# Dividing attention's product with v by the softmax sums, spread over rows by TensorE, in the first five visits

## The chip, the cores and the metric

The kernel runs on one core of a Trainium2 chip. Five engines work side by side, each through its own queue in order: TensorE (PE) multiplies matrices into PSUM, VectorE (DVE), ScalarE (ACT) and GpSimd (POOL) work elementwise (POOL does not read PSUM in this kernel), and SyncE (SP) issues DMA transfers. The metric is the device time of one execution in microseconds; lower is better.

## What is computed

Attention in which a query sees only those keys whose hash (the signs of six random projections) falls into the same bucket, then a two-layer network with squared relu on the joined heads.

```python
q_bits = (np.einsum('bhsd,dk->bhsk', q, proj) > 0).astype(np.int64)
k_bits = (np.einsum('bhsd,dk->bhsk', k, proj) > 0).astype(np.int64)
mask = q_bucket[:, :, :, None] == k_bucket[:, :, None, :]
scores = np.where(mask, scale * np.matmul(q, k.transpose(0, 1, 3, 2)), -1e9)
attn = np.exp(scores - np.max(scores, axis=-1, keepdims=True))
attn = attn / (np.sum(attn, axis=-1, keepdims=True) + 1e-09)
x = np.matmul(attn, v)            # 4 batches, 8 heads, 768 rows, 64 wide
h = np.maximum(x_rows @ w_in, 0)  # x_rows is 3072 x 512, w_in 512 x 2048
out = h * h @ w_out               # w_out 2048 x 512
```

## The kernel before

**Visits and units.** A visit is one batch, one pair of heads and one third (256) of the query rows; there are 48 (line 1039). A visit has four units, one for each head and 128 rows (`unit`, line 877): scores S into PSUM (tiles `pS`, `side`), their maximum on DVE (`line`), the exponential on ScalarE with its row sums (`e`, `sm`), and the sums' reciprocal `rv` (one operation on POOL or DVE, then one on DVE). `prep` (line 782) makes the masked operands A, L, Q, M of a pair of heads from the loaded k and q: a hash on PE (`pd` or `side` with `pj`), its signs `bits` on ScalarE, and rows of mask through PE (`side` or `pc`) that DVE and ScalarE copy to the lower halves of A, L, Q, M.

**Two ways from e to the product with v.** In a plain visit (line 907; `PLAIN_AV`, the first four) e is divided in place by POOL (`move(e, e, rv, ...)`, with `DIVIDE = ("pool",)`), PE transposes it in float32 in two halves (`pT`, against the unit matrix `unit_f`), ScalarE or DVE copies each half to `aT`, and `av` (line 925) multiplies with the float32 V, 12 matmuls with the two heads beside each other. In the other visits e is divided into two float16 parts (`hl`, one on ScalarE and one on DVE, lines 917 and 918), a DMA transpose on SP's queue brings them to `aT`, and `av` takes 36 float16 matmuls with the split `VV`. The product is copied out of the bank `pA` as two float16 parts `xx`.

**The network.** When all four pairs of heads of a third are done, `moe` (line 981) multiplies `xx` with `win` (into `pm`), squares on ScalarE and DVE (`g`), and multiplies with `wo` (into `po`). The weights arrive while the first visits run: `fetch` (line 665) loads a 512-wide block, copies its upper 16 bits (`move(first..., (dve, pool))`, line 671, room<-room in the profile) and joins the lower bits on DVE; `split` (line 692) squares it for a scale (`sq`) and writes two float16 parts into `win` or `wo`.

**What sets the order.** All operations are recorded (`Program.add`) and ordered when the kernel is built. An operation may have several ways, one for each engine that can do it. `forward` takes at each step the operation of the lowest priority number that can start and picks the engine that ends it first by planned costs; the priorities come from a first schedule (`rounds`) and are then changed at random, once for each number in the table `PATH` (`shake`). `SOON` scales the planned duration of transfers until `SOON_TO`. Thus the same operations come out in another order, and partly on other engines, wherever an operation or a number changes. All operations are issued from one helper, line 565 (558 for groups of matmuls, 563 for chains), which is why the profile shows that line for nearly all.

**The tiles of the first units.** `unit_f` is loaded on SP's queue (line 647), and `ident`, a cast of it on DVE (line 649), is needed for the scale of V (`dg`). `idle` are matmuls without use that fill PE's waits at the beginning.

Of the kernel before, what the change touches and what calls it, by code (L numbers as in the profile page):

```python
# [12 lines left out]
F16 = mybir.dt.float16  # L13
BF16 = mybir.dt.bfloat16
# [10 lines left out]
P = 128  # L25
# [24 lines left out]

ROUNDS, BEHIND = 24, 40000
PATH = (
# [13 lines left out]
)  # L66
LOADS = 0

# [3 lines left out]

PLAIN, PLAIN_TO, ALTERNATE, DOUBLE = 4, 12, 16, 34

PLAIN_AV, DIVIDE = (0, 1, 2, 3), ("pool",)

AV_RUN = 18

# [15 lines left out]

SWITCH, ENTRY = 95, 105
TRANSPOSES, HBM, SMALL = 165, 265, 300
SOON, SOON_TO = 0.7, 22000


class Buffer:  # L100
# [477 lines left out]
def lsh_attention_moe(ctx: ExitStack, tc, kq, v, proj2, w_in, w_out, consts, out):  # L578
# [64 lines left out]
    for n in range(4):  # L643
        move(sgn[32 * n : 32 * n + 32, n * P : (n + 1) * P], both_f[0:32, 4:], 1.0, (dve, pool) if n else (dve,))
    pr.rank = 0.0
    unit_f = sb([P, P], F32, "unit_f")
    sp.dma_start(unit_f, consts[:, 4 + 2 * P :])
    ident = sb([P, P], BF16, "ident")
# [16 lines left out]
    def fetch(src):  # L665

        raw = place(turn[0] % 2 * 4096, 4096, U32).rearrange("p (n t) -> p n t", t=2)
        send(raw.rearrange("p n t -> p (n t)").bitcast(U16)[:, 0:2047], src.bitcast(U16)[:, 1:2048])
        first = tops[turn[0] % len(tops)]
        turn[0] += 1  # L670
        move(first[:, :, 1], raw.rearrange("p n t -> p (n t)").bitcast(BF16).rearrange("p (n t) -> p n t", t=4)[:, :, 2], 1.0, (dve, pool))
        f = place(12288 + turned[0] % ((ROOM - 12288) // 2048) * 2048, 2048, F32)
        turned[0] += 1
        dve.scalar_tensor_tensor(f.bitcast(U32), raw[:, :, 0], 13, first.rearrange("p n t -> p (n t)").bitcast(U32), ALU.logical_shift_right, ALU.bitwise_or)
        return f
# [198 lines left out]
        return VV  # L874


    def unit(st, part, i, aT, plain):
        c0 = part * PT + i * P
        u = pr.rank
        if u >= DOUBLE and u % 2:  # L880
            pS = side
        else:
            pS = ps([P, 2, 512], F32, "pS", tag="po" if u % 2 and u < ALTERNATE else "pS")
        pr.marks[u] = len(pr.ops)
        pr.rank = u - 1000
        for s, (a, bb) in enumerate(st):
            for j in range(2):
                pe.matmul(pS[:, j, 0:HS], a[:, c0 : c0 + P], bb[:, j * HS : (j + 1) * HS], start=s == 0, stop=s == len(st) - 1)
        sS = pS[:, 0:2, 0:HS]
        line = lines[int(u) % 2]  # L890
        nmx = line[:, 1:2]
        todo = [("tensor_reduce", (nmx, sS, AX.XY, ALU.max), {"negate": True})]
        to = {"bias": nmx}
        if len(st) > 1:
            pair = sb([P, 2], F32, "pair", 2)
            todo += [("scalar_tensor_tensor", (pair, nmx.broadcast_to([P, 2]), MASK * MASK / 2, line, ALU.is_lt, ALU.mult), {})]
            to = {"scale": pair[:, 0:1], "bias": pair[:, 1:2]}
        pr.add((dve, "chain", todo, {}))
        e = sb([P, S], F32, "e", BUFS["e"])
        sm = sb([P, 1], F32, "sm", 2)  # L900
        act.activation(e.rearrange("p (j s) -> p j s", j=2), sS, AF.Exp, accum_out=sm, **to)
        pr.rank = u
        rv = sb([P, 1], F32, "rv", 3)
        pr.add(*[(q, "tensor_scalar", (rv, sm, 1e-9, 1.0 if plain else 1.0 / ASC, ALU.add, ALU.mult), {}) for q in (dve, pool)])
        dve.reciprocal(rv, rv)
        if plain:
            move(e, e, rv, tuple(getattr(pr, k) for k in DIVIDE))
            for g in range(2):
                pT = ps([P, 512], F32, "pT", tag=("pm", "pA")[g])[:, 0:HS]
                pr.busy_from = min(pr.busy_from, len(pr.ops))  # L910
                for c in range(3):
                    kc = 3 * g + c
                    pe.matmul(pT[:, c * P : (c + 1) * P], e[:, kc * P : (kc + 1) * P], unit_f, start=True, stop=True, is_transpose=True)
                move(aT[:, 3 * g : 3 * g + 3, i * P : (i + 1) * P], pT.rearrange("p (c s) -> p c s", c=3), 1.0, (act, dve))
            return
        hl = sb([P, 2, S], F16, "hl", BUFS["hl"])
        move(hl[:, 0], e, rv)
        left(hl[:, 1], e, rv, hl[:, 0])
        sp.dma_start_transpose(aT[:, :, i * P : (i + 1) * P], hl.rearrange("p t s -> p (t s)"))
# [2 lines left out]

    xxs = {}

    def av(b, hp, part, VV, aTs):
        pA = ps([P, 512], F32, "pA")[:, 0:PT]
        plain = VV.dtype == F32
        todo = [(kc, t * D, kc + l * KC) for t, l in (((0, 0),) if plain else ((0, 0), (1, 0), (0, 1))) for kc in range(KC)]
        scale = vscales[b][0] if plain else 1.0 / ASC
        run = []  # L930
        for n, (kc, d0, c) in enumerate(todo):
            run += [((pA[m], VV[:, h, kc, d0 : d0 + D], aTs[h][:, c]), {"start": n == 0, "stop": n == len(todo) - 1}) for h, m in enumerate((T, U))]
            if (n + 1) % (AV_RUN if not plain else 6) == 0:
                pr.add((pe, "matmuls", run, {}))
                run = []
        xx = xxs[b, part, hp] = sb([P, 2, PT], F16, "xx")
        move(xx[:, 0], pA, scale)
        left(xx[:, 1], pA, scale, xx[:, 0])

# [113 lines left out]
    done, u, stages = {}, 0, 0  # L1053
    for n, (b, hp, part) in enumerate(visits):
        sts, aTs, plain = kept[b, hp], [], n in PLAIN_AV
        for h, st in enumerate(sts):
            aT = sb([P, KC, PT], F32, "aT") if plain else sb([P, 2 * KC, PT], F16, "aT")
            aTs.append(aT)
            for i in range(RT):
                pr.rank = now[0] = u  # L1060
                unit(st, part, i, aT, plain)
                u += 1
        if n + 1 < len(visits):
            ready(*visits[n + 1][:2], u + PREP, n + 1 < PLAIN_TO and visits[n + 1][1] < PLAIN)
        if (b, hp, plain) not in kept_v or not alive([kept_v[b, hp, plain]]):
            pr.rank = u - 2 * RT + PREP
            kept_v[b, hp, plain] = values(b, hp, plain)
        pr.rank = u - 0.5
        av(b, hp, part, kept_v[b, hp, plain], aTs)
        if n in early:  # L1070
            do, j, pr.rank = early[n]
            do(j)
        done[b, part] = done.get((b, part), 0) + 1
        if done[b, part] == H // 2:
            moe(stages, b, part)
            stages += 1
# [35 lines left out]
```

## Time and profile before

| | us |
|---|---|
| median of 3 runs (lowest, highest) | 869.69 (867.09, 871.51) |
| the profiled execution | 867.13 |
| its span, first to last instruction | 865.1 |
| PE, DVE, ACT, POOL busy | 832.1, 661.7, 666.0, 111.5 |

The span is what the trace covers; the execution's own time is 2.0 us longer. Rows of the profile read: line, engine, operation, written tile <- read tiles, shapes, count, then busy time, the mean ns of one, and the engine's idle time just before them with what ended it. A table of windows gives each engine's busy time in a stretch of the span, the granted clock of TensorE (PEclk, 1.00 is full) and the DMA engines' share. In the chain of waits each piece is a start, a length and what ran.

### The profile page before, as it was taken

Reading aid. Unit: us, or ns where it says so; the run is one execution under the profiler, and the core shown is the slowest. Engines: PE = TensorE matmul, PEld = TensorE weight load, DVE = VectorE, ACT = ScalarE, POOL = GpSimd, SP = SyncE. Lnnn points to the kernel's source line nnn. Section 1 sums busy time; section 2 is a strip of 40 time slices with the busy share of each in tenths; the row PEclk is TensorE's granted clock in tenths of the full one; section 3 lists DMA queues with packets and bytes.
Section 4 is the critical chain, followed back from the end, with each engine's and each line's share of the span. In section 5 each row is a group of like instructions: output and inputs, shape, how many; then the busy total and the mean of one; then the engine's idle time right before and its main releaser. Section 6 shows DMA issues by size and latency. Waiting matters only on the chain.

```text
span 865.1 us, 16996 instructions
## 1 busy us (share of the span) xinstructions
PE 832.1 (96%) x6340; PEld 543.8 (63%) x6343; DVE 661.7 (76%) x1448; ACT 666.0 (77%) x1153; POOL 111.5 (13%) x175
## 2 busy tenths in 40 slices
PE   6999978998999999999999999999999999999997
PEld 4555555665566667667666667676666666766664
DVE  4889988999696999877796888885887988871111
ACT  3897867699796888877886898977887888883332
POOL 0554464310010100000000001000100000000000
PEclk8999999999999999999999999999999999999999
DMA  8426979865788898787575978797665798771000
GB/s 298 128 82 185 195 197 226 188 117 108 177 168 189 159 166 163 143 156 169 134 156 153 165 155 146 151 159 164 135 111 157 145 150 150 135 147 38 1 25 25
DMA packets 301634, 125.77 MB, mean 145 GB/s; under 512 B 279792, under 2 KB 287728, under 8 KB 301552
## 3 DMA queue, kind: packets, MB, share of 16 engines
q1 hardware_dynamic: 301264, 124.61, 68.6%
q8 instruction: 50, 0.82, 0.4%
q14 instruction: 32, 0.26, 0.1%
q10 hardware_dynamic: 288, 0.08, 0.0%
HBM read 37.36 MB, written 6.29 MB: 50 GB/s over the span
## 4 chain that ended last, share of the span: by engine, by line
PE 73%; DVE 11%; ACT 8%; issue 3%; DMA 3%; POOL 1%; SPq 0%; ACTq 0%; DVEq 0%; POOLq 0%
PE pm L565 24%; PE po L565 24%; PE pA L558 9%; PE pS L565 8%; PE side L565 6%; DVE line L563 3%; ACT e L565 3%; DVE hl L565 2%; ACT g L565 1%; ACT hl L565 1%; PE pd L558 1%; DMA unit_f<-consts 1%; DMA V<-vp 1%; DVE room L565 1%; PE pc L565 1%
## 5 line engine op out<-in xcount | busy, mean ns | idle before, releaser
L565 PE MATMUL pm<-xx,win 128*128 128x256 f16 x2304 | 308.3, 273 | 3.0 <-DVE g L565 1.2
L565 PE MATMUL po<-wo,g 128*128 128x512 f16 x1152 | 298.7, 379 | 4.7 <-ACT acc L565 3.2
L565 PEld LDWEIGHTS <-win 128*128 128x128 f16 x2304 | 223.0, 98 | 84.0 <-issue 18.0
L565 DVE SCALAR_TENSOR_TENSOR hl<-e,rv,hl 128x768 f16<-128x768 f32 x176 | 179.5, 1025 | 15.8 <-ACT hl L565 14.8
L565 PEld LDWEIGHTS <-g 128*128 128x128 f16 x1152 | 111.4, 98 | 107.6 <-issue 11.2
L565 ACT ACTIVATE hl<-e,rv 128x768 f16<-128x768 f32 x168 | 155.2, 928 | 8.3 <-DVE rv L565 3.8
L563 DVE TENSOR_REDUCE line<-pS 128x1 f32<-128x768 f32 x113 | 107.8, 954 | 21.0 <-PE pS L565 18.9
L565 ACT ACTIVATE g<-g 128x512 f32<-128x512 f32 (+1 forms) x184 | 114.7, 625 | 10.3 <-PE po L565 7.7
L565 POOL TENSOR_SCALAR rv<-sm 128x1 f32<-128x1 f32 x98 | 37.9, 387 | 590.5 <-ACT e L565 558.3
L565 DVE SCALAR_TENSOR_TENSOR g<-g,g 128x512 f16<-128x512 f32 x84 | 57.7, 686 | 69.1 <-ACT g L565 69.0
L565 ACT ACTIVATE g<-pm 128x512 f32<-128x512 f32 x93 | 55.0, 591 | 68.6 <-PE pm L565 68.5
L558 PE MATMUL pA<-aT,VV 128*64 128x256 f16 x1584 | 94.9, 274 | 0.0
L558 PEld LDWEIGHTS <-VV 128*64 128x64 f16 x1584 | 83.1, 110 | 12.9 <-issue 12.5
L565 ACT ACTIVATE e<-pS,pair 128x768 f32<-128x768 f32 x72 | 71.0, 986 | 24.0 <-DVE pair L563 13.8
L565 ACT ACTIVATE e<-side,pair 128x768 f32<-128x768 f32 x72 | 71.0, 986 | 12.6 <-DVE pair L563 7.3
L563 DVE TENSOR_REDUCE line<-side 128x1 f32<-128x768 f32 x79 | 75.2, 951 | 5.0 <-PE side L565 4.0
L565 ACT ACTIVATE e<-pS,line 128x768 f32<-128x768 f32 x41 | 36.9, 899 | 8.3 <-DVE line L563 6.8
L565 PEld LDWEIGHTS <-room 128*128 128x128 f16 x288 | 27.8, 98 | 18.3 <-issue 1.3
L565 PE MATMUL pS<-A,L 128*128 128x384 f32 x84 | 34.9, 529 | 4.6 <-DVE L L565 2.4
L565 PE MATMUL pS<-room 128*128 128x384 f16 x144 | 36.0, 326 | 0.0
L565 PE MATMUL side<-room 128*128 128x384 f16 x144 | 34.6, 326 | 0.0
L565 PE MATMUL pS<-Q,M 128*128 128x384 f32 x80 | 31.3, 503 | 2.5 <-ACT e L565 2.3
(164 smaller groups left out, 905.6 us busy)
## 6 DMA issues: line engine op xcount, KB each, us to landing
R<-kq SPq DMA_DIRECT2D x24, 384.0 KB, 4.1
room<-w_in SPq DMA_DIRECT2D x16, 511.8 KB, 3.9
room<-w_out SPq DMA_DIRECT2D x16, 511.8 KB, 3.7
V<-vp SPq DMA_DIRECT2D x16, 384.0 KB, 4.1
out<-acc SPq DMA_DIRECT2D x24, 256.0 KB, 2.8
room<-room SPq DMA_DIRECT2D x60, 96.0 KB, 2.9
aT<-hl SPq DMA_TRANSPOSE x176, 3.9
Q<-kq SPq DMA_DIRECT2D x6, 384.0 KB, 4.1
```

Source lines behind the costliest of these rows:

```text
L558: ins = q.engine.matmul(*map(real, args), **kw).ins
L563: issue(q, getattr(q.engine, name)(*map(real, args), **{k: real(x) for k, x in kw.items()}).ins)
L565: ins = getattr(q.engine, o.name)(*map(real, o.args), **{k: real(x) for k, x in o.kw.items()}).ins
```

## The change

In the first five visits (the fifth is new: `PLAIN_AV` gets a 4) e goes undivided through the float32 transposes and the product with V. For each unit a diagonal matrix with rv on it is made from `unit_f` (`DIVIDE` is now ScalarE; the four diagonals of a visit lie in one `hl` buffer). In `av`, four float32 matmuls of ones (128 x 64) with the diagonals put each row's reciprocal sum into all 64 partitions of the output, in the free half of the bank `pA`; a copy scales them by V's scale, and DVE multiplies the product with them before it is split into `xx`. The upper-bits copy of a weight block may now also go to ScalarE; second halves of transposes keep `pA`, and from unit 16 on first halves use it too. `SOON` no longer shortens early transfers, and `PATH` is another, longer table (2,564 numbers for 234).

```diff
 PATH = (
-    400004, 400029, 400036, 400042, 400059, 400060, 400072, 400092, 400101, 400104, 400119, 400137, 400139, 400148, 400157, 400162, 400198, 400206,
...
+    1200002, 1200003, 1200004, 1200005, 1200006, 1200007, 1200008, 1200014, 1200015, 1200017, 1200018, 1200019, 1200020, 1200024, 1200029, 1200031,
...
-PLAIN_AV, DIVIDE = (0, 1, 2, 3), ("pool",)
+PLAIN_AV, DIVIDE = (0, 1, 2, 3, 4), ("act",)
...
-SOON, SOON_TO = 0.7, 22000
+SOON, SOON_TO = 1.0, 0
...
+    ones_f = sb([P, D], F32, "ones_f")
+    pool.memset(ones_f, 1.0)
...
-        move(first[:, :, 1], raw.rearrange("p n t -> p (n t)").bitcast(BF16).rearrange("p (n t) -> p n t", t=4)[:, :, 2], 1.0, (dve, pool))
+        move(first[:, :, 1], raw.rearrange("p n t -> p (n t)").bitcast(BF16).rearrange("p (n t) -> p n t", t=4)[:, :, 2], 1.0, (dve, pool, act))
...
-    def unit(st, part, i, aT, plain):
+    def unit(st, part, i, aT, plain, dg=None):
...
-            move(e, e, rv, tuple(getattr(pr, k) for k in DIVIDE))
+            move(dg, unit_f, rv, tuple(getattr(pr, k) for k in DIVIDE))
             for g in range(2):
-                pT = ps([P, 512], F32, "pT", tag=("pm", "pA")[g])[:, 0:HS]
+                pT = ps([P, 512], F32, "pT", tag="pm" if g == 0 and u < 16 else "pA")[:, 0:HS]
...
-    def av(b, hp, part, VV, aTs):
-        pA = ps([P, 512], F32, "pA")[:, 0:PT]
+    def av(b, hp, part, VV, aTs, dgs=None):
+        bank = ps([P, 512], F32, "pA")
+        pA = bank[:, 0:PT]
...
+        if plain:
+            pR, t, rvs = bank[:, PT:], dgs[:, 0:PT], dgs[:, 2 * RT * P :]
+            matmuls(*[(pR[m, i * P : (i + 1) * P], ones_f, dgs[:, (h * RT + i) * P : (h * RT + i + 1) * P]) for i in range(RT) for h, m in enumerate((T, U))])
+            move(rvs, pR, scale, (act, dve))
...
         xx = xxs[b, part, hp] = sb([P, 2, PT], F16, "xx")
+        if plain:
+            dve.tensor_tensor(t, pA, rvs, ALU.mult)
+            move(xx[:, 0], t)
+            left(xx[:, 1], t, 1.0, xx[:, 0])
+            return
         move(xx[:, 0], pA, scale)
         left(xx[:, 1], pA, scale, xx[:, 0])
...
+        dgs = sb([P, 2, S], F16, "hl", BUFS["hl"]).rearrange("p t s -> p (t s)").bitcast(F32) if plain else None
```

Three places show what the order becomes. First, SP's queue at the start of the program, where the loads are issued (A and Q are k and q of a head, V two heads of v, room<-w_in a block of weights). Before:

```order
L565 DMA Q<-kq 128x768
L565 DMA A<-kq 128x768 x2
L565 DMA Q<-kq 128x768
L565 DMA V<-vp 128x768
L565 DMA room<-w_in 128x2047
L565 DMA V<-vp 128x768
L565 DMA room<-w_in 128x2047
L565 DMA V<-vp 128x768 x2
L565 DMA Q<-kq 128x768
L565 DMA A<-kq 128x768
L565 DMA unit_f<-consts 128x128
```

And of the change:

```order
L713 DMA A<-kq 128x768
L713 DMA Q<-kq 128x768 x2
L713 DMA A<-kq 128x768
L713 DMA room<-w_in 128x2047
L713 DMA unit_f<-consts 128x128
L713 DMA room<-w_in 128x2047
L713 DMA V<-vp 128x768 x4
L713 DMA Q<-kq 128x768
```

The load of unit_f stood thirteenth and stands sixth now, ahead of all four loads of v.

Second, DVE's queue in the first two visits' preparation, up to the first maximum (L, M, A, Q<-side are the mask rows, room<-room the join of a weight's bits, line_78 and line_63 the maximum of the first unit). Before:

```order
L565 TENSOR_SCALAR L<-A 64x768
L565 TENSOR_SCALAR M<-Q 64x768
L565 TENSOR_SCALAR A<-side 64x384 x2
L565 TENSOR_SCALAR L<-side 64x384
L565 TENSOR_SCALAR room<-room 128x512
L565 CAST ident<-unit_f 128x128
L565 SCALAR_TENSOR_TENSOR room<-room 128x512
L565 TENSOR_SCALAR Q<-side 64x384
L563 TENSOR_REDUCE line_78<-pS 128x1
```

And of the change:

```order
L713 TENSOR_SCALAR L<-A 64x768
L713 TENSOR_SCALAR M<-Q 64x768
L713 CAST ident<-unit_f 128x128
L713 TENSOR_SCALAR M<-Q 64x768
L713 TENSOR_SCALAR A<-side 64x384 x2
L713 TENSOR_SCALAR L<-A 64x768
L711 TENSOR_REDUCE line_63<-pS 128x1
L713 SCALAR_TENSOR_TENSOR room<-room 128x512
L713 TENSOR_SCALAR Q<-side 64x384 x2
```

The cast that needs unit_f stood between the mask rows and the first maximum; it stands ahead of the mask rows now, and the first maximum follows the mask rows with one copy between.

Third, POOL's queue in the first two visits (e<-e,rv is the division of a unit's weights, sq<-room the square of a weight block). Before:

```order
L565 TENSOR_SCALAR sgn<-cst 32x128
L565 TENSOR_SCALAR room<-room 128x512
L565 TENSOR_SCALAR rv<-sm 128x1
L565 TENSOR_SCALAR e<-e,rv 128x768
L565 TENSOR_SCALAR rv<-sm 128x1
L565 TENSOR_SCALAR e<-e,rv 128x768
L565 TENSOR_SCALAR rv<-sm 128x1
L565 TENSOR_SCALAR dg<-ident,top 128x128
L565 TENSOR_SCALAR room<-room 128x512
L565 TENSOR_SCALAR e<-e,rv 128x768
```

And of the change:

```order
L713 TENSOR_SCALAR sgn<-cst 32x128
L713 TENSOR_SCALAR rv<-sm 128x1
L713 TENSOR_TENSOR sq<-room 128x512
L713 TENSOR_SCALAR rv<-sm 128x1
L713 TENSOR_SCALAR M<-Q 64x768
L713 TENSOR_SCALAR dg<-ident,top 128x128
L713 TENSOR_SCALAR L<-A 64x768
L713 TENSOR_SCALAR rv<-sm 128x1
L713 TENSOR_SCALAR room<-room 128x512
```

No division is left on POOL, and copies of k and q that stood on ScalarE and DVE have come to it; over the whole program its room<-room go from 26 to 12, while ScalarE gets 17 of them, 20 diagonals (hl<-unit_f,rv) and five copies of the spread sums (hl<-pA,tov). DMA transposes go from 176 to 172, float32 transposes on PE from 96 to 120, DVE's hl<-e,rv,hl from 176 to 172, and DVE's hl<-e,rv from seven to three.

More of the change, by code (lines that the diff above doesn't have):

```diff
@@ L1060, in lsh_attention_moe @@
                 pr.rank = now[0] = u
-                unit(st, part, i, aT, plain)
+                unit(st, part, i, aT, plain, dgs[:, (h * RT + i) * P : (h * RT + i + 1) * P] if plain else None)
                 u += 1
@@ L1068, in lsh_attention_moe @@
         pr.rank = u - 0.5
-        av(b, hp, part, kept_v[b, hp, plain], aTs)
+        av(b, hp, part, kept_v[b, hp, plain], aTs, dgs)
         if n in early:
```

172 rows, old and new, of the table PATH are left out of this document.

## The prediction

> **What bounds the kernel now.** I read the page's busy table first, then the table of windows, then the chain of work that ended last, and last the engines' instructions in order of time around the places which those name.
>
> ```profile
> PE 832.1 (96%) x6340; PEld 543.8 (63%) x6343; DVE 661.7 (76%) x1448; ACT 666.0 (77%) x1153; POOL 111.5 (13%) x175
> ...
> core 0: us, PE busy (x) PEld busy (x) DVE busy (x) ACT busy (x) POOL busy (x), PEclk, DMA share, GB/s
> 0.00:11.00 11.00, 7.22 (x80) 6.03 (x80) 5.47 (x21) 3.94 (x6) 0.70 (x6) 1.00 0.83 296
> 11.00:22.00 11.00, 6.23 (x15) 2.97 (x15) 3.59 (x8) 4.53 (x9) 0.95 (x2) 0.69 0.78 291
> 22.00:84.00 62.00, 56.73 (x318) 32.56 (x320) 56.03 (x124) 54.22 (x109) 32.26 (x43) 1.00 0.43 123
> 84.00:160.00 76.00, 68.71 (x457) 42.90 (x457) 70.09 (x134) 57.59 (x101) 37.39 (x42) 1.00 0.91 209
> 160.00:200.00 40.00, 37.74 (x267) 23.05 (x264) 37.92 (x77) 33.74 (x56) 5.83 (x11) 1.00 0.80 153
> 200.00:840.00 640.00, 634.86 (x5084) 423.72 (x5083) 485.04 (x1084) 504.19 (x864) 34.34 (x71) 1.00 0.71 139
> 840.00:865.10 25.10, 20.56 (x131) 12.53 (x128) 3.52 (x5) 7.74 (x13) 0.00 (x0) 0.99 0.06 22
> ```
>
> TensorE is the bound: from 200 us on it rests 5.1 of 640 us, so whatever PE work the change adds is paid there unless a rest elsewhere takes it up. The rests lie early: 8.6 us up to 22, 5.3 us from 22 to 84, and 76.0 - 68.7 + 40.0 - 37.7 = 9.6 us from 84 to 200. In these stages DVE is as full as PE (56 of 62, then 108 of 116 us), so PE waits there for chains through DVE, ScalarE and the loads. The tail after the last matmul stays as it is.
>
> **The start.** The changed order moves the load of unit_f ahead of all of V.
>
> ```profile
> 8.93 0.56 DVE L565 TENSOR_SCALAR M<-Q 64x768 f32<-64x768 f32 x1 [0.46 <-DMA Q<-kq]
> 9.50 1.02 DVE L565 TENSOR_SCALAR A<-side 64x384 f32<-64x384 f32 x2
> ...
> 17.32 0.23 DVE L565 CAST ident<-unit_f 128x128 bf16<-128x128 f32 x1 [5.70 <-DMA unit_f<-consts]
> ...
> 18.76 0.96 DVE L563 TENSOR_REDUCE line<-pS 128x1 f32<-128x768 f32 x1
> ...
> 11.14 1.41 PE L565 MATMUL pS<-A,L 128*128 128x384 f32 x2 [2.45 <-DVE L L565]
> ...
> 12.67 1.49 PE L565 MATMUL pS<-A,L 128*128 128x384 f32 x2
> ...
> 9.87 0.84 ACT L565 ACTIVATE sqv<-V 128x768 bf16<-128x768 f32 x1 [3.00 <-DMA V<-vp]
> ...
> 12.15 0.84 ACT L565 ACTIVATE sqv<-V 128x768 bf16<-128x768 f32 x1 [0.38 <-DMA V<-vp]
> ...
> 19.90 0.90 ACT L565 ACTIVATE e<-pS,line 128x768 f32<-128x768 f32 x1
> ...
> 13.49 0.76 POOL L565 TENSOR_SCALAR room<-room 128x512 f16<-128x512 bf16 x1 [8.40 <-DMA room<-w_in]
> ```
>
> The first scores are done at 12.67 + 1.49 = 14.2, yet DVE takes their maximum only at 18.76: it stands 5.70 us in its own queue behind a cast that needs unit_f. In the new order unit_f is SP's sixth load, behind the four of q and k and one of w_in. Q, the fourth, landed at 8.93; between 9.87 and 12.15 a w_in and a V came, 512 + 384 KB, 0.39 KB/ns, so w_in would land at 10.2 and unit_f (64 KB) at 10.4; bounds are 8.93 and the 13.49 at which a load of w_in that stood eighth was waited for. From 10.4 the new DVE order runs the cast (0.23), M<-Q (0.56), two A<-side (1.02 both) and the scores follow: start at 12.1, 2.9 us as now, maximum at 15.0. That is **3.8 us earlier** than 18.76, with bounds of 0.7 (unit_f at 13.49) and 5 (unit_f at 8.93). Hidden behind nothing: all chains start from it.
>
> **What the arithmetic adds and removes.**
>
> ```profile
> L565 PE MATMUL pT<-unit_f,e 128*128 128x128 f32 x96 | 15.9, 277 | 1.5 <-ACT aT L565 1.2 <-POOL e L565 0.2
> ...
> L558 PE MATMUL pA<-aT,V 128*64 128x256 f32 x96 | 11.2, 383 | 0.0
> ...
> L558 PE MATMUL pA<-aT,VV 128*64 128x256 f16 x1584 | 94.9, 274 | 0.0
> ...
> L565 DVE SCALAR_TENSOR_TENSOR hl<-e,rv,hl 128x768 f16<-128x768 f32 x176 | 179.5, 1025 | 15.8 <-ACT hl L565 14.8
> ...
> L565 DVE TENSOR_SCALAR hl<-e,rv 128x768 f16<-128x768 f32 x7 | 4.3, 615 | 0.1
> ...
> L565 DVE SCALAR_TENSOR_TENSOR xx<-pA,xx 128x256 f16<-128x256 f32 x44 | 18.4, 418 | 13.5 <-ACT xx L565 13.3
> ...
> L565 ACT ACTIVATE dg<-ident,top 128x128 bf16<-128x128 bf16 x3 | 1.2, 397 | 0.0
> ...
> L565 ACT ACTIVATE xx<-pA,tov 128x256 f16<-128x256 f32 x2 | 0.9, 474 | 0.8 <-PE pA L558 0.7
> ...
> L565 ACT ACTIVATE aT<-pT 128x384 f32<-128x384 f32 x31 | 14.1, 491 | 0.5 <-PE pT L565 0.4
> ...
> L565 ACT ACTIVATE sq<-room 128x512 bf16<-128x512 f32 x28 | 16.9, 625 | 9.6 <-DVE room L565 6.5 <-DVE rv L565 1.7 <-DVE norm L565 1.3
> ...
> L565 POOL TENSOR_SCALAR e<-e,rv 128x768 f32<-128x768 f32 x16 | 17.0, 1064 | 15.4 <-DVE rv L565 10.0 <-PE side L565 1.7 <-DVE fromwin L565 1.4
> ...
> L565 POOL TENSOR_SCALAR room<-room 128x512 f16<-128x512 bf16 x26 | 24.8, 963 | 14.2 <-DMA room<-w_in 10.6 <-DMA room<-w_out 2.9
> ...
> L565 DVE TENSOR_SCALAR room<-room 128x512 f16<-128x512 bf16 x6 | 2.9, 481 | 0.1
> ```
>
> PE. The fifth visit gets 24 transposes: a quarter of 15.9 us is 4.0; that share holds pipeline ends which overlap other work in the mixed order, so I take 3.0 (bounds 2.0 and 4.0). Its product with v goes from 94.9 / 44 = 2.16 to 11.2 / 4 = 2.80 us, +0.6. The sums spread over rows are new: four f32 products a visit, two heads beside each other, half as wide as the twelve that cost 2.80, so 2.80 x 4 / 12 / 2 = 0.47 us, five times 2.3 (nothing makes it a gain; as 20 separate ones of 0.277, the mean of one transpose, it would be 5.5). **PE: +5.9 us**, bounds 4.5 and 10. No visit is taken off PE for it, so it is paid in full.
>
> DVE loses, by the counts of the order, four of the 1.025 and four of the 0.615 (6.6 us) and gets five products of pA with the spread sums (0.42 each, as the row of xx) and small copies that came over from other engines: by counts times such means some 2 us less in all. ScalarE gets 20 diagonals (0.397: 7.9 us), five copies of the sums (0.474: 2.4), 17 room copies (the nearest row is 0.625: 10.6) and five more aT (2.5), and by the counts gives 14 other copies back, some 9 us: +14 us. In the stages up to 160 us it rests 138 - 111.8 = 26 us, which hides that if it falls between the exponentials. POOL loses all 16 divisions and 14 of its 26 room copies, 30 us; the divisions stood between each exponential and its transposes, and PE waited 1.5 us for transposes. With transposes taking e undivided, I take **-1.0 us** for the stage from 22 to 84 (bounds 0 and -3; the exponentials themselves come no sooner there, since DVE, by the order's counts times the means of the groups, an estimate, has some 8 us more work in front of the sixteenth maximum than before, moved forward from later).
>
> The new wait: dg, the copy of the sums and one DVE product stand in front of the xx of each plain visit, and the pA bank is held that much longer, so second halves of transposes queue behind it. PE has scores of the next units between, and xx is needed only by the pm of a whole stage; I take 0, and 5 x 0.5 = 2.5 us if the cover goes.
>
> **The stage with the weights** (84 to 200) has the longest chain off PE.
>
> ```profile
> 102.51 5.34 DMA room<-w_out
> ...
> 108.00 1.00 POOL room L565
> 109.00 1.49 issue
> ...
> 157.31 2.18 POOL wo L565 x2
> 159.49 1.85 issue
> ...
> L565 SPq DMA_TRANSPOSE aT<-hl x28: 1275/1485/3538, 79.6 to 196.6; - x28
> ...
> 143.31 1.56 PE L565 MATMUL pS<-Q,M 128*128 128x384 f32 x4 [1.66 <-ACT e L565]
> ```
>
> Before the next matmul, chains pass a load of w_out of 5.3 us, POOL copies of 1.00 and 2.18 us and 3.3 us behind them. The change takes four DMA transposes out of SP's queue here (4 x 1.485 = 5.9 us, of a stage with a DMA share of 0.91), halves POOL's copies, gives them to an engine that does one in about 0.63 for 0.96 us, and takes six microseconds off DVE in this very visit. Of the 9.6 us that PE rests I take half, **-4.8 us** (bounds +2, where PE waits for exponentials behind room copies, and -8). What is late next is an exponential behind ScalarE's own queue, as at 143.31.
>
> [...]
>
> Later than 200 us the same instructions stand in another order, from the long list of numbers; PE's 5.1 us of rest there may shrink or grow by some 3. I take 0.
>
> **Sum.** -3.8 + 5.9 - 1.0 - 4.8 = -3.7 us against the profiled execution, 867.13 us with a span of 865.1 and 2.0 around it, which is the lowest of the three shown. Taken off the median of 869.69 it gives **866.0**.
>
> **Rivals.**
> - *The weights' stage opens up.* If loads, POOL and DVE were the whole of PE's rest there, 7.5 of the 9.6 us go and 3 of the 5.3 before: -3.8 + 5.9 - 3.0 - 7.5 = -8.4, 861.3. For it: the DMA share of 0.91 and the POOL pieces on the chain. Against: DVE stays at over 100 of 116 us.
> - *PE's work is paid and nothing given back* (slower). Place: ScalarE between the exponentials up to 160 us. With 14 us more there and 8 us more on DVE ahead of the sixteenth maximum, the lead of the start is eaten by 84 us, and exponentials come behind room copies as often as they come earlier. Price: +5.9, 875.6. It decides from where ScalarE's 26 us of rest turn out to be waits that its chains need; its 57.6 of 76 us speak against, its 54.2 of 62 for.
> - *The start does not come.* Were unit_f still late (13.49), the first maximum gains 0.7 instead of 3.8, and the sum is -0.6: 869.1. Or PE had no use for the divisions on POOL: the change would do what it says and shorten nothing.
>
> **Chances.** The forecast (863 to 868.5 its own range) 0.40; the stage opens up 0.29; paid in full 0.18; the start does not come 0.13. A measurement of this kernel tells about 0.5%, 4.35 us, from no change: faster means under 865.3, slower over 874.0. Of the forecast 0.14 lies under 865.3; of the slower case 0.05 lies within. Faster 0.43, same 0.44, slower 0.13. The range leaves out the far ends of the two outer cases: 858 to 874.
>
> **What would show it.** In the changed profile the cast of ident should begin near 10.4 and the first maximum near 15.0; PE's total should be 836 to 841 us; POOL 80 to 88 us; PE's rest from 84 to 200 about 5 us and ScalarE some 165 us busy up to 200, where it is 154 now. Wrong would be a first maximum later than 17, PE waits for ACT e of more than 8 us, or rests after 200 of over 8 us. The whole falls if the reordering, not the arithmetic, moved the end.

## The result and the profile after the change

The changed kernel takes **879.27 us** (median; 877.30 to 879.57), the kernel before 868.98 over four executions, three of which are those of the table of before. The ratio is **1.0116 [1.0098, 1.0133]**: 10.3 us slower, outside the predicted range of 858 to 874. One execution of experiment 9 took 2226.66 us and is left out of its numbers below; its other eleven lie between 869.40 and 873.89.

The profiled execution has a span of 877.3 us, 12.2 more than before. First its busy table on the page, then the table of windows by stage (columns as in the prediction's; PEclk is the number behind POOL's).

```profile
PE 839.1 (96%) x6394; PEld 548.0 (62%) x6394; DVE 663.1 (76%) x1450; ACT 676.1 (77%) x1180; POOL 86.9 (10%) x161
```

```profile
0.00:22.00 22.00, 15.99 (x120) 10.66 (x121) 12.74 (x34) 9.88 (x18) 2.04 (x9) 0.92 0.91 333
22.00:84.00 62.00, 54.39 (x324) 30.89 (x323) 55.85 (x130) 54.71 (x121) 20.88 (x32) 1.00 0.38 116
84.00:200.00 116.00, 106.87 (x699) 67.02 (x698) 99.93 (x192) 92.81 (x162) 32.55 (x50) 0.97 0.75 168
200.00:840.00 640.00, 629.19 (x5049) 419.03 (x5047) 489.65 (x1089) 507.17 (x862) 31.48 (x71) 1.00 0.72 140
```

A span is TensorE's busy time plus its rests, so the 12.2 us can be split. A stage's length less PE's busy time is its rest; before, these are 8.55, 5.27, 9.55 and 5.14 us by the prediction's rows. After the change they are 6.01, 7.61, 9.13 and 10.81, and the page's PE total grows by 7.0: -2.5 + 2.3 - 0.4 + 5.7 + 0.1 behind 840 + 7.0 = 12.2. Two of these are a surprise. From 84 to 200 us PE rests as long as before, although the stage lost transposes, GpSimd copies and six microseconds of DVE; and PEclk there is 0.97.

The timeline shows where. Rows have the start, the duration, the engine and its line, the operation, and in brackets the idle time ahead and what ended it; SPq is SyncE's queue of DMA issues.

```profile
105.02 0.33 SPq L713 DMA_DIRECT2D room<-w_in  x1
116.42 0.33 SPq L713 DMA_DIRECT2D V<-vp  x1
116.85 0.39 SPq L713 DMA_DIRECT2D room<-w_in  x1
...
115.35 1.01 DVE L713 SCALAR_TENSOR_TENSOR VV<-V,tov,VV 128x768 f16<-128x768 f32 x1
...
122.24 0.69 DVE L713 SCALAR_TENSOR_TENSOR room<-room 128x512 uint32<-128x512 uint32 x1 [5.80 <-ACT room L713]
...
115.01 0.62 ACT L713 ACTIVATE sq<-room 128x512 bf16<-128x512 f32 x1
121.43 0.77 ACT L713 ACTIVATE room<-room 128x512 f16<-128x512 bf16 x1 [5.81 <-DMA room<-w_in]
...
124.08 0.58 PE L713 MATMUL side<-sq,ones 128*128 128x512 bf16 x1 [5.08 <-ACT sq L713]
...
127.09 2.76 PE L713 MATMUL pS<-Q,M 128*128 128x384 f32 x4
```

Read it upwards. PE stands 5.08 us for a square that ScalarE does late, because ScalarE has stood 5.81 us ahead of a copy of a w_in block, because that block's load was issued only at 116.85. It was issued so late because the entry ahead of it in SyncE's queue, a load of V for the second batch, was held from about 105 to 116.42. The waits of SyncE's queue from 84 to 200 us name the releaser (total, times, longest):

```profile
SPq L713 <- DVE VV L713: 19.1, 2, 11.0
```

The split of VV on VectorE ends at 116.36, and the load of V goes out 0.06 us later. V and VV share one set of buffers, so a load of V has to wait until an older tile of the set has been read for the last time. Before the change the same two loads of V were SyncE's 51st and 52nd entries; after it they are the 42nd and 48th, ahead of loads of weights that are wanted at once.

The rest costs a second time. The windows around it:

```profile
118.00:124.00 6.00, 1.00 (x6) 0.36 (x4) 1.76 (x3) 2.57 (x5) 1.16 (x2) 1.00 1.05 281
124.00:130.80 6.80, 5.95 (x14) 2.92 (x14) 3.76 (x8) 4.38 (x8) 2.26 (x4) 0.50 0.50 134
```

For 6.8 us behind the rest, PE ran at a granted clock of 0.50: four products of scores took 2.76 us there, against 1.56 for four at full clock (143.31 in the prediction's rows). PE was busy for 5.95 of these 6.8 us, and from 131.2 to 132.0 us the granted clock was 1.00 again.

### The profile page after: what moved, and what is told of

Read it like the earlier page. It is cut to its first block, busy times and chain, and to the rows that moved or that the text cites. A ratio compares the mean times of both kernels' runs of the same rounds, so it can differ in the third digit from the quotient of the medians.

```text
span 877.3 us, 17105 instructions
## 1 busy us (share of the span) xinstructions
PE 839.1 (96%) x6394; PEld 548.0 (62%) x6394; DVE 663.1 (76%) x1450; ACT 676.1 (77%) x1180; POOL 86.9 (10%) x161
## 5 line engine op out<-in xcount | busy, mean ns | idle before, releaser
L713 DVE SCALAR_TENSOR_TENSOR hl<-e,rv,hl 128x768 f16<-128x768 f32 x172 | 175.1, 1023 | 21.5 <-ACT hl L713 20.1
L713 ACT ACTIVATE g<-g 128x512 f32<-128x512 f32 (+1 forms) x176 | 109.4, 625 | 14.4 <-PE po L713 12.0
L706 PE MATMUL pA<-aT,VV 128*64 128x256 f16 x1548 | 93.0, 274 | 0.3 <-DMA aT<-hl 0.3
L706 PEld LDWEIGHTS <-VV 128*64 128x64 f16 x1548 | 81.3, 110 | 14.8 <-issue 13.9
L713 POOL TENSOR_SCALAR rv<-sm 128x1 f32<-128x1 f32 x98 | 34.0, 347 | 559.6 <-ACT e L713 559.3
L713 ACT ACTIVATE e<-pS,pair 128x768 f32<-128x768 f32 x72 | 71.0, 986 | 14.1 <-DVE pair L711 11.6
```

Source lines behind the costliest of these rows:

```text
L706: ins = q.engine.matmul(*map(real, args), **kw).ins
L713: ins = getattr(q.engine, o.name)(*map(real, o.args), **{k: real(x) for k, x in o.kw.items()}).ins
```

## The experiments

In all of them the operations of the changed kernel (or, in one, of the kernel before) keep the planner's order and engine, except for what the edit names; it stands behind the line that asks the planner for the order. A pair (i, j) takes operation i out and puts it right behind j. Ratios are against the kernel before, 868.3 to 868.7 us in these runs. Differences between two kernels are taken from the medians; worked out from the ratios they come out up to 1.8 us otherwise, and both are given where that matters.

**1. Both loads of V later.** 2175 and 2177 are the two loads, 813 and 816 two loads of w_out.

```diff
         out = self.order()
+        for i, j in ((2175, 813), (2177, 816)):
+            out.remove(i)
+            out.insert(out.index(j) + 1, i)
```

> The kernel after the change, with two loads of SyncE's queue moved: the two loads of V for the second batch, which stood at 116.42 and 132.25 us, are issued some twelve entries later, behind two loads of w_out. Nothing else moves. Theory A (the load of V, waiting for a split of VV late in VectorE's queue, holds a load of w_in behind it, and ScalarE's copy of that load holds the exponentials): the 5.8 us wait of ScalarE near 121 us and the 5.1 us wait of TensorE near 124 us go, the granted clock stays at 1.0 there, and the time falls by about 8 us, to 871 (869 to 873). Rival B (TensorE is in any case late there, because VectorE's and ScalarE's queues are full between 84 and 124 us; the wait moves on to the next entry): the time stays within 2 us of 879.3.

Measured: **867.80 us, 0.9998 [0.9989, 1.0007]**, 11.5 us under the changed kernel. By the ratios it is 10.2 us. The timeline of this run there, and its windows:

```profile
104.32 5.17 SPq L716 DMA_DIRECT2D room<-w_in  x2
...
119.72 0.59 PE L716 MATMUL po<-wo,g 128*128 128x512 f16 x2 [0.78 <-ACT acc L716]
```

```profile
0.00:22.00 22.00, 17.34 (x123) 11.72 (x124) 12.84 (x34) 10.57 (x20) 2.04 (x9) 0.92 0.89 332
22.00:84.00 62.00, 54.39 (x324) 30.83 (x322) 55.98 (x130) 54.34 (x121) 21.15 (x33) 1.00 0.37 120
84.00:200.00 116.00, 111.68 (x754) 71.44 (x754) 107.59 (x205) 101.61 (x171) 35.13 (x49) 1.00 0.79 181
200.00:840.00 640.00, 632.08 (x5070) 421.42 (x5069) 483.57 (x1077) 502.58 (x862) 30.66 (x71) 1.00 0.70 137
```

Theory A holds, with more gained than the 8 us it expected. The rest from 84 to 200 falls from 9.13 to 4.32 us, PEclk there is 1.00, and PE's total falls by 3.1 to 836.0 us. That is 7.9 of the 12.1 us between the spans. Another 2.9 come after 200 us (rest 7.92 for 10.81) and 1.4 at the start, where no instruction was moved. Neither of these two is shown to follow from the stall: the kernel of experiment 2 keeps the stall, and PE rests only 640 - 632.20 = 7.80 us there after 200 us.

**2. Copies back from ScalarE to GpSimd**, the stall left as it is.

```diff
         out = self.order()
+        for i in (143, 140, 258, 386, 514, 539, 545, 658, 661, 664, 667, 692, 695, 701, 811, 814, 820):
+            o = self.ops[i]
+            o.queue, o.name, o.args, o.kw = next(w for w in o.ways if w[0].key == "pool")[:4]
```

> The kernel after the change with the 17 copies out of the loaded weights that ScalarE does before 150 us given to GpSimd, at the same places of the order; all else as it is. Theory A (the load of V blocks the load of w_in; what makes it a wait of TensorE is that the copy stands between exponentials in ScalarE's queue): ScalarE no longer waits for a load near 121 us, the 5.8 us wait goes over to GpSimd and to VectorE's join behind it, and TensorE still waits some 3 to 5 us there through VectorE; the time falls by 0 to 4 us. Rival B (ScalarE as third choice for copies is the fault by itself, 17 times 0.77 us in an engine full of exponentials): the time falls by 6 us or more, to 873 or less.

Measured: 879.98 us, 1.0141 [1.0120, 1.0162], no gain. The wait moved as A said, and whole:

```profile
122.60 0.76 POOL L716 TENSOR_SCALAR room<-room 128x512 f16<-128x512 bf16 x1 [6.12 <-DMA room<-w_in]
...
123.39 1.05 DVE L716 SCALAR_TENSOR_TENSOR room<-room 128x512 uint32<-128x512 uint32 x1 [5.84 <-POOL room L716]
...
125.22 0.59 PE L716 MATMUL side<-sq,ones 128*128 128x512 bf16 x1 [5.32 <-ACT sq L716]
```

For the stall it does not matter whether ScalarE or GpSimd copies: VectorE's join behind the copy holds everything else in VectorE's queue (5.84 us here, 5.80 with ScalarE), and PE waits 5.32 us (5.08 with ScalarE).

**3. The order of the kernel before from about 270 us on.** TAIL is a table of the last 5137 operations with their engines.

```diff
         out = self.order()
+        out = out[: len(out) - len(TAIL)] + [n >> 3 for n in TAIL]
+        for n in TAIL:
+            o = self.ops[n >> 3]
+            o.queue, o.name, o.args, o.kw = next(w for w in o.ways if w[0].key == ("pe", "dve", "act", "pool", "sp")[n & 7])[:4]
```

> The kernel after the change up to some 270 us, and from there the order (and choice of engine for each copy) of the kernel before, as a table of the same 5137 operations. Theory A (the order found by the new list of numbers is worse on the chip after 200 us, where TensorE loses 14.6 us against 7.9 us before): the time falls by 3 to 6 us, to 873 to 876. Rival B (the late losses follow from the state that the early stages leave behind, such as fewer weights prepared or fewer units ahead): the time stays within 1.5 us of 879.3.

Measured: 875.87 us, 1.0092 [1.0076, 1.0109], 3.4 us under the changed kernel (2.1 by the ratios): A's 3 to 6 us by the medians, between A and B by the ratios.

**4. Both edits, 1 and 3.**

> Both edits at once: the two loads of V later, and the order of the kernel before from some 270 us on. If the two losses are separate, their gains add up: 8 us and 3 to 6 us off 879.3, so 865 to 868, which is 1 to 4 us under the kernel before. If the stall before 124 us and the late order are one loss seen twice (the late order suffers from being late), the sum is less than the two gains, by 2 us or more.

Measured: 866.86 us, 0.9980 [0.9971, 0.9990]. Beside edit 1 the older order is worth 0.9 us (1.6 by the ratios). So the late order costs something, some 1 to 3 us; whether the gains add up is not decided, since they do by the ratios and fall short by 2.5 us by the medians.

**5. The split earlier instead of the load later.** 1210 is VectorE's half of the split, 1096 the reciprocal at 108.01 us.

```diff
+        for i, j in ((1210, 1096),):
```

> The kernel after the change with one instruction moved: VectorE's half of the split of VV that ended at 116.36 us stands fourteen entries earlier in VectorE's queue, behind the reciprocal at 108.01 us. The load of V keeps its place in SyncE's queue. Theory A (the load of V waits for this split, and the split is late only because VectorE's queue is behind): the load of V is issued near 109 us instead of 116.42, SyncE's longest wait falls from 11 to 3 or 4 us, ScalarE's 5.8 us wait nearly goes, and the time comes within 3 us of the 867.8 us that moving the loads gave; the second load of V may still cost 1 or 2. Rival B (the load waits for something else, such as an earlier transfer or a product with v): the load stays near 116 us and the time within 2 us of 879.3.

Measured: 869.62 us, 1.0014 [1.0005, 1.0024].

```profile
109.87 0.33 SPq L716 DMA_DIRECT2D V<-vp  x1
...
108.84 1.00 DVE L716 SCALAR_TENSOR_TENSOR VV<-V,tov,VV 128x768 f16<-128x768 f32 x1
```

The load follows the split wherever the split stands (108.84 + 1.00, load at 109.87), and 9.7 of the 11.5 us (8.9 of 10.2 by the ratios) come back without a change to SyncE's queue. This settles the releaser.

**6. Only the first load of V later**, to directly ahead of the second.

```diff
+        for i, j in ((2175, 691),):
```

> The kernel after the change with only the first of the two loads of V moved, five entries later, to directly ahead of the second, which stays where it was (issued at 132.25 us after a wait of 8 us). Theory A (the first load alone makes the stall of TensorE at 124 us): 867 to 870. Rival B (the second load, which waits too, takes the first one's place, holding the transposes and the loads of w_out behind it): 872 to 879, with a wait of SyncE of over 5 us and one of ScalarE or VectorE behind it.

Measured: 869.70 us, 1.0014 [1.0004, 1.0023]. The first load makes the stall; the second costs some 2 us more (1.4 by the ratios).

**7 and 8. The copies on GpSimd and on VectorE, without the stall**: edit 1 with edit 2, the second time with "dve" for "pool".

> The two loads of V later (867.8 us by itself), and the 17 copies of loaded weights that ScalarE does before 150 us given to GpSimd. Theory A (with no load late, ScalarE has room for the copies, and where they are done costs nothing that TensorE sees): within 2 us of 867.8. Rival B (the copies hold exponentials; without them ScalarE runs ahead): 863 to 865. Rival C (GpSimd's copies are slower, 0.96 us for 0.77, and VectorE's joins behind them come later): 869 to 873.

> The two loads of V later (867.8 us by itself), and the 17 copies given to VectorE, where one takes 0.48 us. [...] By the windows VectorE is the fuller engine (55.9 of 62 us, then some 71 of 76), and 17 times 0.48 is 8.2 us more for it, on the chain between scores and exponentials: 869 to 876. [...]

Measured: on GpSimd 871.29 us, 1.0035 [1.0022, 1.0048]; on VectorE 870.95 us, 1.0029 [1.0018, 1.0039]. Both are over 3 us more than with ScalarE (867.80), or 3.2 and 2.7 by the ratios. So A of experiment 7 fails and its C holds, and 8 came out as I expected.

**9. The products that spread the sums, twice** (with edit 1).

```diff
-                for args, kw in o.args:
+                for args, kw in o.args * (2 if len(o.args) == 4 and o.args[0][0][1].shape == o.args[0][0][2].shape[:1] + (64,) and o.args[0][0][2].shape[1:] == (128,) else 1):
```

> The two loads of V later (867.8 us by itself), and each of the five plain visits issues its four products that spread the sums over rows twice, the second time over the same result. In the changed kernel's trace these products are busy 3.3 us in all. Theory A (TensorE is the bound in these visits, its added work is paid in full): 3.3 us more, 871.1 (870 to 872). Rival B (TensorE rests in these visits anyway, waiting for ScalarE and VectorE, and the work falls into the rests): within 1 us of 867.8.

Measured: 871.25 us, 1.0029 [1.0017, 1.0041], 3.5 us over edit 1 alone between the medians, 2.7 by the ratios; 3.3 was expected. PE's total is 839.3 us, 3.3 over that of edit 1. TensorE's work in these visits is paid, in full as far as these numbers go.

**10. The old start in the changed kernel** (with edit 1). 13 is the load of unit_f, 14 its cast, 233 and 102 a load of A and the copy of L.

```diff
+        for i, j in ((2175, 813), (2177, 816), (14, 102), (13, 233)):
```

> The two loads of V later (867.8 us by itself), and the load of unit_f put back to the thirteenth place of SyncE's queue, the cast of ident behind L in VectorE's: the start of the kernel before. The first maximum falls back from 14.9 to 18 or 19 us. Theory A (the lead of the start is carried to the end): 3 to 4 us more, 871 to 872. Rival B (the lead is eaten by 60 us, where the milestones of the two kernels meet, because VectorE has more in front of the exponentials): within 1 us of 867.8.

Measured: 870.81 us, 1.0024 [1.0013, 1.0035], 3.0 us more than edit 1 (2.3 by the ratios). The first maximum stood at 18.15 us. The start is worth about what the prediction gave it.

**11. The kernel before with one load moved.** 12 is its load of unit_f, 98 the last of the first four loads of q and k.

```diff
         out = self.order()
+        for i, j in ((12, 98),):
+            out.remove(i)
+            out.insert(out.index(j) + 1, i)
```

> The kernel before the change with one load moved: unit_f is SyncE's fifth load, behind the four of q and k, instead of its thirteenth. The first maximum should come near 14.5 us instead of 18.76. Theory A (each microsecond at the start is one at the end): 3.5 to 4.3 us less, 864 to 865. Rival B (the lead is lost at the next bound, DMA or VectorE): within 1 us of 868.4.

Measured: **861.24 us, 0.9914 [0.9898, 0.9929]**, 7.3 us under the kernel before: faster than both kernels, and twice what A expected. VectorE's queue at the start, and the windows:

```profile
10.15 0.21 DVE L568 CAST ident<-unit_f 128x128 bf16<-128x128 f32 x1
...
11.60 0.96 DVE L566 TENSOR_REDUCE line<-pS 128x1 f32<-128x768 f32 x1
```

```profile
0.00:22.00 22.00, 18.19 (x132) 12.04 (x133) 16.71 (x42) 14.92 (x28) 5.41 (x14) 1.00 0.90 352
22.00:84.00 62.00, 57.49 (x330) 33.32 (x332) 55.97 (x123) 55.13 (x109) 31.93 (x42) 1.00 0.46 136
84.00:200.00 116.00, 106.12 (x740) 66.80 (x738) 109.04 (x211) 91.97 (x152) 39.10 (x49) 1.00 0.80 176
200.00:840.00 640.00, 633.36 (x5058) 422.13 (x5057) 478.67 (x1071) 499.77 (x859) 34.30 (x71) 1.00 0.70 139
```

The cast no longer makes VectorE wait, and the first maximum comes at 11.60, 7.16 us earlier than 18.76. I had expected 14.5, from the changed kernel's 14.85, and overlooked that there the cast stands ahead of M and A:

```profile
9.33 0.23 DVE L713 CAST ident<-unit_f 128x128 bf16<-128x128 f32 x1 [2.71 <-DMA unit_f<-consts]
9.57 0.56 DVE L713 TENSOR_SCALAR M<-Q 64x768 f32<-64x768 f32 x1
...
14.85 0.96 DVE L711 TENSOR_REDUCE line<-pS 128x1 f32<-128x768 f32 x1 [3.11 <-PE pS L713]
```

**12. The changed kernel with both: V later, and the better start.**

```diff
+        for i, j in ((2175, 813), (2177, 816), (13, 98), (14, 102)):
```

> The changed kernel with the two loads of V later (867.8 us by itself), the load of unit_f at SyncE's fifth place instead of its sixth, and the cast of ident behind the two A and one L of VectorE instead of ahead of M. In the changed kernel VectorE rests 2.71 us for that cast; without it the first maximum should come near 12 us instead of 13.9. Theory A (a lead at the start is carried to the end in the changed kernel too): 1.5 to 2.5 us less, 865 to 866. Rival B (the changed kernel's VectorE is so full from 22 to 84 us that it eats the lead): within 1 us of 867.8.

Measured: 866.26 us, 0.9960 [0.9944, 0.9976], 1.5 us under edit 1 by the medians and 3.3 by the ratios, so A holds with its size open. The first maximum came at 11.03 us for edit 1's 13.87. Its windows:

```profile
0.00:22.00 22.00, 17.98 (x136) 12.26 (x137) 15.68 (x40) 13.68 (x28) 3.03 (x11) 1.00 0.92 347
22.00:84.00 62.00, 55.08 (x333) 31.75 (x332) 55.68 (x130) 54.47 (x120) 21.49 (x32) 1.00 0.36 120
84.00:200.00 116.00, 110.76 (x748) 70.38 (x746) 107.98 (x206) 101.83 (x169) 34.00 (x47) 1.00 0.79 179
200.00:840.00 640.00, 631.27 (x5061) 420.54 (x5062) 480.55 (x1074) 499.88 (x858) 30.90 (x71) 1.00 0.70 137
```

## Why the prediction was wrong

TensorE's rests by stage, worked out from the rows above and the prediction's (stage less PE busy; the last row of rests is what is left of the span), and PE's busy total on each page:

| us | before | changed | 1: V later | 11: before, unit_f early | 12: changed, V later, unit_f early |
|---|---|---|---|---|---|
| rest 0 to 22 | 8.55 | 6.01 | 4.66 | 3.81 | 4.02 |
| rest 22 to 84 | 5.27 | 7.61 | 7.61 | 4.51 | 6.92 |
| rest 84 to 200 | 9.55 | 9.13 | 4.32 | 9.88 | 5.24 |
| rest 200 to 840 | 5.14 | 10.81 | 7.92 | 6.64 | 8.73 |
| rest behind 840 | 4.5 | 4.6 | 4.7 | 4.5 | 4.7 |
| PE busy | 832.1 | 839.1 | 836.0 | 829.5 | 834.7 |
| span | 865.1 | 877.3 | 865.2 | 858.8 | 864.3 |

Columns 11 and 12 have nearly the same start, a full clock and no stall of V, so between them stands the change without the stall and without a late cast, though still with its own order elsewhere: slower by 5.5 us in the spans, 5.0 in the medians, 4.0 by the ratios.

**The step that failed** is in the stage with the weights: "What is late next is an exponential behind ScalarE's own queue". What was late next was a load of w_in behind a load of V in SyncE's queue. I counted the four transposes that left that queue and not the load of V that moved forward in it, past weights, to a place where its buffer was not yet free. Its price, by experiment 1, is 11.5 us (10.2 by the ratios). Of this 7.9 us are located in the trace: 4.8 us of rest from 84 to 200 us, where the wait of 5.08 us stood, and 3.1 us of PE's work, which ran at the halved clock behind it. What is left is not traced to the stall. Neither bounds (+2 to -8) nor rivals held it.

Point by point:

- *The start, -3.8: right.* The cast began at 9.33 (10.4 forecast), the first maximum at 14.85 (15.0). The nearness is partly luck. The cast came 1.1 us earlier than forecast, but ScalarE's copy to L, which the sum left out, stands between VectorE's A (done at 11.16) and the first scores at 11.88 (12.1 forecast):

```profile
11.25 1.04 ACT L713 ACTIVATE L<-side,floor 64x384 f32<-64x384 f32 x2 [4.05 <-DVE A L713]
...
11.88 2.93 PE L713 MATMUL pS<-A,L 128*128 128x384 f32 x4 [3.31 <-ACT L L713]
```

  The lead was carried to the end: experiment 10 gives 3.0 us (2.3 by the ratios) for taking it back. I didn't see that the new place of the cast makes VectorE wait 2.71 us for it, which experiment 12 removes.
- *TensorE's work, +5.9: right in sum*, 5.2 by PE's totals in columns 11 and 12 (the total of the changed kernel itself, +7.0, holds the halved clock). The single terms were all low. The groups of the changed kernel, with their total and mean:

```profile
L706 PE MATMUL pA<-aT,VV 128*64 128x256 f16 x1548 | 93.0, 274 | 0.3 <-DMA aT<-hl 0.3
...
L713 PE MATMUL pT<-unit_f,e 128*128 128x128 f32 x120 | 20.8, 278 | 1.3 <-ACT e L713 0.8 <-ACT aT L713 0.4
...
L706 PE MATMUL pA<-aT,V 128*64 128x256 f32 x120 | 14.1, 383 | 0.6 <-ACT hl L713 0.6
...
L706 PE MATMUL pA<-hl,ones_f 128*64 128x128 f32 x40 | 3.3, 285 | 0.0
```

  Transposes grew by 20.8 - 15.9 = 4.9 (3.0 forecast), the products with v by 14.1 - 11.2 - 94.9 + 93.0 = 1.0 (0.6), and the sums take 3.3 (2.3). Groups overlap (those of PE in the changed kernel add up to 1036.0 us, for 839.1 busy), so these 9.2 us are more than the total gained. That added work of this kind is paid and not hidden is shown by experiment 9.
- *22 to 84 us, -1.0: wrong sign.* The rest there grew by 2.3 (2.4 between columns 11 and 12). The term itself came true: PE's waits for transposes in this stage fell by 1.0 us. Before (total, times, longest):

```profile
PE pT L565 <- ACT aT L565: 1.2, 2, 0.9
...
PE pT L565 <- POOL e L565: 0.2, 1, 0.2
```

  and after the change:

```profile
PE pT L713 <- ACT aT L713: 0.4, 1, 0.4
```

  But the new order put other waits in their place, for which the sum had no term: the hash of the next heads (side<-A,pj) waits until the last mask rows M of the heads before it have been copied out of `side`. Before the change it started without such a wait:

```profile
33.30 0.52 PE L558 MATMUL side<-A,pj 128*32 128x384 f32 x2
...
44.23 0.52 PE L558 MATMUL side<-A,pj 128*32 128x384 f32 x2 [0.20 <-DVE norm L565]
```

  and after the change:

```profile
29.12 0.52 PE L706 MATMUL side<-A,pj 128*32 128x384 f32 x2 [1.83 <-DVE M L713]
...
43.34 0.52 PE L706 MATMUL side<-A,pj 128*32 128x384 f32 x2 [0.91 <-ACT M L713]
```

  These two waits, 2.7 us, stand in column 1 too (1.8 and 0.9), and the first of them in column 12 (1.8). No run moved them, so that the whole 2.3 us hang on them is read from the trace and not tried. The exponentials did come no sooner there, as the prediction said: the first is 4.06 us earlier than before (15.84 for 19.90), the sixteenth 1.87 later. Before:

```profile
70.93 0.90 ACT L565 ACTIVATE e<-pS,line 128x768 f32<-128x768 f32 x1
```

  and after the change:

```profile
72.80 0.90 ACT L713 ACTIVATE e<-pS,line 128x768 f32<-128x768 f32 x1
```

  The prediction had some 8 us more of VectorE's work ahead of that one and gave them no price.
- *84 to 200 us, -4.8: the size comes out without the stall, the mechanism only in part.* Without the stall the rest falls by 5.2 (before to column 1) or 4.6 (columns 11 to 12); the changed kernel itself shows -0.4. The half that I took of the 9.6 us was a choice and not worked out from a wait, so its nearness is partly luck. PE's longest waits in this stage before were for exponentials, and none was directly for a load or a copy of POOL's:

```profile
PE pS L565 <- ACT e L565: 3.3, 4, 1.7
```

  In column 1 no wait for an exponential is left in this list, whose first line is

```profile
PE po L716 <- DVE rv L716: 0.8, 1, 0.8
```

  Of the four reliefs that the prediction names, only the copies were tried: with them on GpSimd (experiment 7) the rest is 116 - 108.99 = 7.01 us in place of 4.32.
- *The new wait at dg, 0: right.* The products pA<-aT,V waited 0.6 us in all for ACT hl (the row above).
- *After 200 us, 0: wrong*, +5.7 in the changed kernel. It is 2.9 less in column 1, but not by the stall alone, as experiment 2 shows. The prediction took 0 for the new order without a reason. Between columns 11 and 12 it costs 2.1 us. The trace names waits of PE for transfers between operands (A<-A, L<-A and Q<-Q), of 2.4 us in all in the changed kernel and 1.3 in column 1, where the kernel before has none. What makes them late is open: the older order from 270 us on gives 0.9 to 1.6 us beside edit 1, and kernels with one and the same order after 200 us differ by more (rest 7.92 in 1, 9.92 in 9).
- *The rivals.* "PE's work is paid and nothing given back", 875.6, came nearest in number, but not by its mechanism: it blamed copies on ScalarE between exponentials, and taking them off gained nothing (experiment 2) or lost over 3 us (7 and 8). On VectorE they cost 3.1 us more than on ScalarE (experiment 8; 2.7 by the ratios); VectorE was busy 107.59 of 116 us from 84 to 200 even without them. The price of a copy on ScalarE was too low: 0.778 us measured, for the 0.625 of the nearest row.
- *The signs.* PE's total of 839.1 and POOL's 86.9 us lie in their forecast ranges, PE's also without the 3.1 us of the stall (836.0 in column 1). ScalarE was busy 157.4 us up to 200 (some 165 forecast) and 166.5 in column 1. Of the signs of being wrong, one appeared: a rest after 200 us of over 8.

Term by term without the stall (column 1 less the column before, the forecast in brackets): start -3.9 (-3.8), PE busy +3.9 (+5.9), 22 to 84 +2.3 (-1.0), 84 to 200 -5.2 (-4.8), behind 200 +3.0 (0). That is +0.1 where the sum said -3.7, and a time of 867.8 where it said 866.0: two terms of the sum were wrong (22 to 84 us by +3.3, after 200 by +3.0), a smaller PE term took back 2.0 of that, and the stall, which had no term, made the miss.

## What to carry to other kernels

When an order changes, walk each DMA queue entry by entry and ask of every load that moved forward which instruction frees its buffer and how late that one stands on its own engine: all entries behind it wait as well (here a load of w_in, issued at 116.85 behind the load of V at 116.42). Move such a load back or its releaser forward; here either was worth some 9 to 11.5 us. And compare an arithmetic change with the old arithmetic at an equally good order: the gain that came with this one, an early load of unit_f, was worth 7.3 us by itself, and against the old arithmetic with that load in place the change is 4 to 5 us slower (its own order elsewhere included).

## What the runs showed of the hardware that I had not expected

One rest is paid twice: after 5.08 us without a matmul the granted clock was 0.50 for 6.8 us, and PE's total fell by 3.1 us when the rest was removed. At the start of the kernel before the clock was 0.69 from 11 to 22 us, for 1.00 in experiment 11, which is a part of what that experiment won: its PE total is 2.6 us lower, with the same instructions.

With each engine's order fixed, a shift at the start was carried almost unchanged through the first 170 us. In experiment 12 against experiment 1, the first exponential is 2.84 us earlier (12.02 for 14.86), the sixteenth 3.24 (68.86 for 72.10) and the fortieth 3.22 (171.32 for 174.54); 1.5 us (medians) to 3.3 (ratios) of it are left in the time. Between those points nothing in this kernel absorbed the lead.
